# Two DMA issues behind ScalarE's first copies, and one load to the end of its row in SyncE's queue

## The chip, the cores and the metric

The kernel runs on one core of one Trainium2 chip. A core has TensorE (PE, its weight loads shown apart as PEld), VectorE (DVE), ScalarE (ACT), GpSimd (POOL) and SyncE (SP), which work on their own programs and wait for each other by semaphores. DMAs are issued here by SP, ACT and POOL. The metric is the device time of one execution in microseconds (us), the median of several runs.

## The reference

Inputs are `q, k, v, a_re, a_im` of shape (4, 8, 768, 48), that is batch, heads, steps and head size, and two weights of a gated layer. The first half is linear attention with a complex decay per step and channel:

```
a    = (a_re + i*a_im) * min(|a|, 0.999) / (|a| + 1e-6)
S_t  = a_t * S_(t-1) + k_t v_t^T          (S is 48 x 48 per head, complex)
y_t  = q_t . Re(S_t)
```

The second half takes `x = y` as 3072 rows of 384 and computes `h = x @ w_in` (384 x 2048), `g = h * cos(h)` and `g @ w_out` (2048 x 384). The output is 3072 x 384 in float32. The weights come as 64-bit floats and are converted on the chip.

## The kernel before

The 3072 steps are 24 chunks of 128 steps, and two chunks are one group (`G = 2`), so there are 12 groups. Within a chunk the decay is turned into sums: the logarithms of the magnitudes (`lg`) and the angles (`tan`, later the phases) are summed along the steps by a product with a triangular matrix (`p_powers`, `g_phase`). The exponentials of the sums are the powers `P` and `Q = 1/P`. Keys are multiplied by `Q` and queries by `P`, and both by the cosine and the sine of the phase (`p_apply`, `g_stack`): these are the turned keys `ks` and queries `qs`, 96 wide. Then the chunk is ordinary attention: scores of `ks` and `qs`, masked by the causal triangle (`f_scores`, written to `atm`), times `v`, plus the queries times the `state` carried from the chunk before (`f_rows` or `f_out`). The state of the next chunk is `sp`, the keys times the values (`state_sums`), scaled by the chunk's last power (`state_next`).

That last power is called the *end*. It is the last row of `P` in a tile that has steps as partitions, and it is needed with channels as partitions. `row_out` writes the row (3 KB) to a buffer in DRAM by one DMA, and `row_back` reads it back into `end` by two DMAs, the upper and the lower 48 partitions, element by element. For group 0 ACT's queue issues all three (`scalar` in the calls), for later groups SP's. `p_end` scales `end` on DVE and folds it into the test value `least`; `state_next` then uses it.

For groups 0 and 1, `f_turn` turns keys and queries on PE by transposes into a bank of PSUM (`tp`, four heads each), and ACT copies each bank out to `kT` or `qT`. `turn(g, i)` does four of these for one chunk: two for `kT` and two for `qT`. From group 2 on, DVE's block transposes and SP's DMAs do this instead.

The weights are converted in pieces: POOL's queue issues a DMA into `raw`, ACT scales the low words (`lows`), and DVE does three steps per piece (`piece`). The gated layer of a group follows as `hp` (first product), `gate` (cosine and product) and `op` or `sum` (second product).

The order of the instructions: for PE, POOL and the special functions of ACT the order is that of the program text throughout. For DVE and the rest of ACT, including what ACT's queue issues through `scalar`, it is that of the text through the opening of the kernel (`Ordered.by_hand = "vector", "scalar"`); a helper records each such instruction, which is why many have line 676, 687 or 707. The instructions of SP's queue are ordered by a scheduler, unless `behind(a, b)` puts `a` after `b` on their common engine without a wait. The loads of the opening (`load`, line 584) are recorded without such an order, and so is the constant `sums_turned`, which POOL's `exact` is copied from. Each group's `re`, `im`, `k` and `q` share one buffer per name, while `v` has two.

```
DMA             before: waits for the landing of        after: waits for the landing of
v(0) a, b       re(0) a, im(0) a                        re(0) a, im(0) a
sums_turned     v(0) b                                  re(0) b
row<-lg         k(0) b                                  q(0) a
end<-row, 1st   row, v(1) a                             row, v(0) b
end<-row, 2nd   v(1) b                                  im(1) a
```

The opening around the change runs: logarithms and powers of group 0 by halves, `row_out`, phases, `row_back`, turned keys and queries of both chunks, `turn(0, 0)`, `lows(0, 1)`, `piece(0)`, scores of chunk 0, `turn(0, 1)`, scores of chunk 1, and then the logarithms of group 1 interleaved with the rest of group 0.

## Time and profile before

| | us |
|---|---|
| median of 3 runs (657.73 to 659.49) | 657.82 |
| the profiled execution | 657.8 |
| its span, first to last instruction | 656.0 |
| PE busy | 641.3 (98%) |
| DVE busy | 492.4 (75%) |
| ACT busy | 392.5 (60%) |
| POOL busy | 32.0 (5%) |
| granted clock of TensorE, mean | 0.998 |

Times in the traces count from the start of the span. In a timeline each line has start, length, engine, line of the kernel, operation, output and input tiles, shape and count; in brackets stands how long the engine was idle before it, and what ended that. `SPq` and `ACTq` are the issues of SP's and ACT's queues: their length is that of the issue, not of the transfer. The chain of waits is followed back from the last instruction, at each step to what released it. PE's busy time counts overlapped matrix products and is no measure of its peak.

### The profile page before, as it was taken

To read this page: it belongs to the slowest core of one execution; us is meant where nothing else is said; L and a number is where in the kernel's file an instruction comes from. 1 tells how busy PE (TensorE), PEld (TensorE's weight loads), DVE (VectorE), ACT (ScalarE), POOL (GpSimd) and SP (SyncE) were. 2 spreads that over 40 slices of the span, in tenths; PEclk is the share of its full clock that TensorE was granted. 3 is DMA by queue.
4 is the path that set the end of the run, shared out by engine and by line. 5 is a ranking of instruction groups with operands and counts; after the bars stand their busy time and mean duration, and the time that the engine had idled before them with its cause. 6 is when DMAs were issued, how large, how long until landed. Compare 5 with 4: busy or idle time off the path is not lost.

```text
span 656.0 us, 10759 instructions
## 1 busy us (share of the span) xinstructions
PE 641.3 (98%) x4075; PEld 575.7 (88%) x4075; DVE 492.4 (75%) x799; ACT 392.5 (60%) x726; POOL 32.0 (5%) x53
## 2 busy tenths in 40 slices
PE   8899999999999999999999999999999999999996
PEld 5688867777999899899899899899899999999996
DVE  6899989878687688786787777876877878862251
ACT  7788687293583594494585485485476476433330
POOL 4010100000000010010010010000000000000000
PEclk9999999999999999999999999999999999999999
DMA  9969664727626757737838736836936853364001
GB/s 239 224 187 219 196 189 102 190 60 181 145 49 151 186 135 157 193 98 167 217 78 182 206 92 160 207 95 133 245 104 133 224 127 94 112 135 119 25 1 31
DMA packets 232920, 94.90 MB, mean 145 GB/s; under 512 B 208701, under 2 KB 221246, under 8 KB 232858
## 3 DMA queue, kind: packets, MB, share of 16 engines
q1 hardware_dynamic: 225320, 68.51, 45.9%
q0 software_dynamic: 5824, 25.50, 11.9%
q8 instruction: 34, 0.56, 0.4%
q10 hardware_dynamic: 1714, 0.11, 0.2%
q14 instruction: 28, 0.23, 0.1%
HBM read 69.28 MB, written 24.81 MB: 143 GB/s over the span
## 4 chain that ended last, share of the span: by engine, by line
PE 86%; DMA 6%; SPq 2%; DVE 2%; ACT 2%; issue 1%; ACTq 0%; DVEq 0%
PE hp L687 34%; PE op L687 16%; PE sum L687 15%; PE sc L687 6%; PE yp L687 6%; PE sp L687 4%; DMA v<-in_v_dram 2%; PE phs L687 2%; SPq L584 1%; DMA xT<-x 1%; PE lgs L687 1%; DMA qT<-moved 1%; DMA x<-yT 1%; PE yr L687 1%; SPq L936 1%
## 5 line engine op out<-in xcount | busy, mean ns | idle before, releaser
L687 PE MATMUL hp<-xT,w_in 128*128 128x256 f32 (+1 forms) x1176 | 252.7, 376 | 1.0 <-DMA xT<-x 1.0
L687 PEld LDWEIGHTS hp<-xT,w_in 128*128 128x128 f32 x1176 | 219.9, 190 | 31.5 <-DMA xT<-x 0.9
L707 ACT ACTIVATE gate<-hp,half_pi_b 128x512 f32<-128x512 f32 x96 | 66.0, 687 | 120.2 <-PE hp L687 120.2
L676 DVE TENSOR_TENSOR gate<-hp,gate 128x512 f32<-128x512 f32 x96 | 65.7, 685 | 47.2 <-ACT junk L676 47.1
L687 PE MATMUL op<-w_out,gate 128*128 128x192 f32 (+1 forms) x448 | 100.7, 375 | 0.0
L687 PEld LDWEIGHTS op<-w_out,gate 128*128 128x128 f32 x448 | 76.0, 190 | 16.8 <-issue 2.0
L676 ACT ACTIVATE junk<-hp 128x512 bf16<-128x512 f32 x96 | 56.6, 590 | 0.0
L687 PE MATMUL sum<-t_s,s 128*128 128x192 f32 x320 | 56.3, 329 | 0.0
L687 PEld LDWEIGHTS sum<-t_s,s 128*128 128x128 f32 x320 | 52.1, 190 | 1.5 <-issue 1.5
L676 DVE TENSOR_TENSOR atm<-sc,causal 128x512 f32<-128x512 f32 x48 | 32.9, 688 | 25.7 <-PE sc L687 25.6
L687 PEld LDWEIGHTS sc<-qT,kT 96*128 96x128 f32 x384 | 47.2, 192 | 5.4 <-ACT qT L676 2.5
L687 PE MATMUL sc<-qT,kT 96*128 96x128 f32 x384 | 49.2, 277 | 2.5 <-ACT qT L676 2.3
L676 ACT ACTIVATE ot<-sum 128x192 f32<-128x192 f32 x40 | 12.8, 322 | 52.8 <-PE sum L687 52.6
L676 DVE SCALAR_TENSOR_TENSOR ot<-op,ot 128x192 f32<-128x192 f32 x41 | 13.6, 353 | 39.5 <-PE op L687 37.9
L687 PE MATMUL yp<-atm,v 128*48 128x128 f32 x352 | 33.6, 277 | 0.9 <-ACT Q L707 0.6
L703 ACT ACT_TABLE_LOAD x24 | 30.8, 1283 | 1.1 <-PEq L1657 0.7
L687 PE MATMUL yp<-qT,state 96*48 96x128 f32 x304 | 29.7, 272 | 0.0
L687 PE MATMUL sum<-w_out,gate 128*128 128x192 f32 x160 | 29.7, 330 | 0.0
L687 PE MATMUL sp<-v,ks 128*96 128x48 f32 x320 | 29.7, 246 | 0.0
L687 PEld LDWEIGHTS sp<-v,ks 128*96 128x96 f32 x320 | 29.6, 165 | 0.0
L676 ACT COPY yT<-yp 48x512 f32<-48x512 f32 x44 | 25.2, 573 | 7.4 <-PE yp L687 6.9
L676 ACT CAST tan<-phs 128x384 int32<-128x384 f32 x24 | 11.4, 482 | 29.4 <-PE phs L687 29.4
(145 smaller groups left out, 985.7 us busy)
## 6 DMA issues: line engine op xcount, KB each, us to landing
moved<-tr SPq DMA_DIRECT2D x20, 768.0 KB
raw<-in_moe_w_in_dram POOLq DMA_DIRECT2D x16, 768.0 KB, 5.3
raw<-in_moe_w_out_dram POOLq DMA_DIRECT2D x16, 768.0 KB, 4.9
kT<-moved SPq DMA_DIRECT2D x40, 192.0 KB
qT<-moved SPq DMA_DIRECT2D x10, 768.0 KB
k<-in_k_dram SPq DMA_DIRECT2D x24, 192.0 KB
q<-in_q_dram SPq DMA_DIRECT2D x24, 192.0 KB
v<-in_v_dram SPq DMA_DIRECT2D x24, 192.0 KB
```

The lines of the kernel that those rows point to most:

```text
L584: put(out=tile_[lo:hi, i_], in_=steps[lo + by:hi + by, i_])
L676: ins = getattr(self.engine, op)(**kw)
L687: chain(nc.tensor.matmul(out, **kw), "tensor")
L703: chain(nc.scalar.preload_act_table_set(table))
L707: chain(nc.scalar.activation(func=func, **kw))
L936: nc.sync.dma_start(out=X[g][name][:, ds(i * H, n * H), q4], in_=moved[q4])
```

## The change

In ACT's program the two `end<-row` issues of group 0 move from between the last sine of group 0 and the first `kT` copy to behind the four copies of `turn(0, 0)`, ahead of the two `raw` activations of `lows(0, 1)`. In SP's program the two loads of `v` of group 1 move from behind `v` of group 0 to behind `q` of group 1; `sums_turned` then stands ahead of `im` of group 1 instead of behind `re`. The order on PE, DVE and POOL is the same as before. No instruction is added and none is removed.

```diff
-    load(1, ("re", "im", "k", "q", "v"))
+    load(1, ("re", "im", "k", "q"), put=lambda **kw: late.update(load=nc.sync.dma_start(**kw)))
+    load(1, ("v",), put=lambda **kw: behind(nc.sync.dma_start(**kw), late["load"]))
     ones = constant(sums_np[1], "sums_turned", nc.sync, stage["pool"])
...
     g_trig(0, 1, 1)
-    row_back(0, 0, G, scalar)
     busy(10)
     g_stack(0, 0, 1)
     p_apply(0, 1, 1)
...
     turn(0, 0)
+    row_back(0, 0, G, scalar)
     lows(0, 1)
     piece(0)
```

## The prediction

> **What bounds the kernel now.** I read the page first: PE is busy for 98% of the span, so only an idle stretch of PE, or of what feeds it, is worth anything. I then looked at who waited for whom on PE. The longest single wait of the run, after which nothing is left to make it up, is 2.3 us before the first scores `sc`. Then came the chain of waits in order of time, for the stretch that leads to it:

> ```profile
> 10.88 12.75 DMA v<-in_v_dram
> 23.63 0.02 issue
> 23.65 0.31 ACTq L676
> 23.96 0.04 issue
> 24.00 1.07 ACT kT L676 x2
> 25.06 0.50 ACT qT L676
> 25.56 0.04 issue
> 25.60 2.05 PE sc L687 x16
> ```

> The columns are start and length in us. The start of the kernel hangs on a load of values (`v`), then on a DMA that ACT's own queue issues (`ACTq`), then on ACT's copies of the turned keys and queries, then on PE's scores. The timeline of the same stretch names them:

> ```profile
> 21.30 1.08 PE L948 MATMUL tp<-ident,ks 128*96 128x128 f32 x8 [0.22 <-DVE ks L676]
> 22.24 1.08 PE L948 MATMUL tp<-ident,qs 128*96 128x128 f32 x8
> 22.93 1.02 ACTq L676 DMA_DIRECT2D end<-row  x2
> 24.00 1.07 ACT L676 COPY kT<-tp 96x512 f32<-96x512 f32 x2 [3.01 <-DMA v<-in_v_dram]
> 24.96 1.08 ACT L676 COPY qT<-tp 96x512 f32<-96x512 f32 x2
> 25.91 1.91 ACT L676 ACTIVATE raw<-raw,carrier_b 128x768 uint32<-128x768 uint32 x2
> 26.80 0.69 DVE L676 TENSOR_TENSOR atm<-sc,causal 128x512 f32<-128x512 f32 x1 [1.33 <-PE sc L687]
> 27.69 0.69 DVE L676 TENSOR_TENSOR atm<-sc,causal 128x512 f32<-128x512 f32 x1 [0.20 <-PE sc L687]
> 28.13 1.07 ACT L676 COPY kT<-tp 96x512 f32<-96x512 f32 x2 [0.31 <-PE tp L948]
> 34.79 0.96 DVE L676 SCALAR_TENSOR_TENSOR mag<-re,mag 128x768 f32<-128x768 f32 x1 [0.21 <-ACT mag L707]
> 35.91 0.56 DVE L676 TENSOR_SCALAR lg<-lg 128x768 f32<-128x768 f32 x1 [0.15 <-ACT rs L707]
> ```

> The transposes `tp` of chunk 0 are ready from about 21.9, yet ACT copies them only at 24.00: the two `end<-row` issues stand ahead of the copies in its program. In the built program each DMA of SP and ACT takes one of eight completion semaphores in turn and waits for the DMA that had it before. So the first `end<-row` waits for the written row and for half of the second group's values, and the second one for the other half, which the profile names as releaser. How long such a load takes is read from the packets by queue. In the stretch from 18 to 19 us (packets, MB, share of 16 engines):

> ```profile
> q0 software_dynamic: 101, 0.35, 94.5%
> q1 hardware_dynamic: 102, 0.02, 10.3%
> ```

> q0 is POOL's weights, q1 SP's loads. While the weights move, until about 20.7, SP gets some 100 small packets a us; from 21.0 to 21.5 it got 617. A load has 1024 (128 partitions by 8 heads).

> [...] the row's packets pass between 20.6 and 20.8 and its reader starts at 22.93; the second half of `v` passes its last packet near 21.9 (12,429 packets by 22.0; it is the 12th load, ending at 12,288) and releases at 23.63, which is 1.75 us. [...] the `row<-lg` issue starts at 16.95, ahead of the `below` activation of 17.15 that precedes it in the program.

> **Part one, `row_back` behind `turn(0, 0)`.** It adds nothing; two DMA issues move past four copies.
> - ACT's copies: for chunk 1, when ACT waited for PE, the copy started 0.64 us after the first transpose (27.49 to 28.13). So the first copy goes to 21.30 + 0.64 = 21.94. Two copies take 0.96 (24.00 to 24.96), so the first `qT` starts at 22.90 (its transposes allow 22.24 + 0.64 = 22.88), ACT is free at 23.86, and `sc` starts 0.64 after that `qT` as now (24.96 to 25.60): 23.54. **Gain on PE: 25.60 - 23.54 = 2.06 us.**
> - The two issues, 0.31 us each: the first needs the row (22.9 as now) and the first group's values (tenth load, packets passed by 12.0). The second needs, after the change, the first half of `im` of group 1. That is issued at 13.95 in both (DVE reads the old `im` until 13.85). With no `v` ahead of it, it sends perhaps 500 packets by 20.7 at the shared rate, and the other 520 at 617 per 0.5 us take 0.4: last packet 21.2, landed 22.95. If the copies only stand in ACT's queue, both issues run at 22.9 to 23.4 beside them and cost nothing. If the issues follow the last copy in time, they take two times 0.31 plus two gaps of 0.04, 0.7 us. I take nothing; the trace shows this for one queued instruction only, so I keep both ends.
> - Behind them stand `raw` (two, 1.91) and the copies of chunk 1. At nothing: `raw` 23.9 to 25.8; chunk 1's transposes follow `sc` on PE at 27.49 - 2.06 = 25.43, so the copies start at 26.07, and all of ACT moves by 2.06. At 0.7: `raw` ends at 23.86 + 0.7 + 1.91 = 26.47, and ACT moves by 28.13 - 26.47 = 1.66.
> - DVE: it is idle 1.33, 0.20, 0.12 (31.55 to 31.67), 0.21 and 0.15 between 25.5 and 35.9, 2.01 in all; after 36.4 it works without a gap to 62. Its work from 24.91 cannot come sooner, so these gaps are what it can give. The first `atm` can start at 25.4 (instead of 26.80), the second at 26.0, the conversion behind it at 26.65 instead of 28.30 (1.65); the three later gaps close to about 2.06, since successive starts leave 0.05 to 0.1 more than the ends show. So DVE just follows ACT, with hardly a margin.
> - The ends themselves: scatters of 2 x 768 four-byte packets. They pass now by 27.1 (1,557 of q10 by 27.0), landed near 29. They are issued at the same time or 0.4 us later; DVE's `end` scaling, the first reader, moves from 33.75 to 31.7. Over 2 us remain.
> - From 36 on every wait is on another engine of the same core, and PE is full from 62: the gain goes through to the end. I take off 0.05 for the margin on DVE: **-2.0 us**.

> **Part two, the second group's `v` behind its `q`.** The same bytes in another order; the sums for `exact` now also stand ahead of `im`. `v` is first read by chunk 2's `sp` at 66.18; all loads of group 1 have passed by 32.0, so it lands near 34, and 30 us hide it. In SP's queue it now inherits the waits of `k` and `q` (DVE's reads at 22.65 and 23.1) and of `re`; what is queued behind it, the third group's `v`, is issued at 40.66 and waits for PE. `exact` on POOL comes earlier, but POOL's next weights wait for DVE at 30.98 anyway: nothing. The real effect is cover: `re` of group 1 is the 16th load, its last packet passes at 26.1 (16,297 by 26.0) and it lands near 27.85. ACT will want it at 30.04 - 2.06 = 27.98, so part one alone would have 0.1 us to spare. With `v` out of the way it lands about two loads (1.8 us) sooner. Worth: 0, as cover. Done alone, it would give at most the 0.7 us by which 22.95 is earlier than 23.63.

> **Sum.** The profiled execution took 657.8 us (span 656.0 and 1.8 around it), the median of the three runs is 657.82, so either base serves: 657.8 - 2.0 = 655.8. A difference of 0.3%, 1.97 us, is about what a measurement of this kernel can tell from none, and my number lies at that edge.

> **Rivals.**
> 1. ACT pays for the issues, or `im` is late. For it: only one case of running ahead is seen. If `im` came no sooner than its present packets (13,312th near 22.8, landed 24.55), the second issue ends at 24.86, `raw` at 26.8, a move of 1.35. Against: two loads fewer ahead of it. Gain 1.35 to 1.7: 656.1 to 656.5.
> 2. DVE becomes the bound: if its gaps don't close after 28.30, the move stays at 1.65, or at 1.4 if the first `atm` sets it: 656.15 to 656.4. For it: no slack. Against: ACT, not DVE, ended the later gaps.
> 3. Almost nothing arrives, because group 1's logarithm waits for `re` or a later transfer at a fixed time absorbs it: 657 to 657.8. Against: none of the later waits on PE exceeds 1 us.
> 4. Slower: the scatter of `end` meets the next weights. POOL's next load is issued near 29. If 768 of its packets were still waiting then, they would go at the 100 a us seen above, 7.7 us. It would land near 31 + 7.7 + 1.75 = 40.4; DVE, in order, would stand from 31.7 until then, 8.7 us, and the net is 8.7 - 2.0 = +6.7: 664.5. It decides once packets pass later than 29.9; slower than now once they pass later than 32. Against: 27.1 now.

> **How the numbers follow.** The main case (gain 1.85 to 2.15) has 0.60, of which 0.45 over the edge of 1.97 and 0.15 under; rivals 1 and 2 have 0.24, rival 3 has 0.07, rival 4 has 0.05, and 0.04 goes to a gain beyond 2.15. Faster by over 0.3%: 0.49. Within: 0.46. Slower: 0.05. The range of 655.2 to 657.0 takes the main case, rivals 1 and 2, and the noise of the times, and leaves out rival 4, most of rival 3 and the extremes. The main case alone is 655.6 to 656.0.

> **What would show it.** Right: first `kT` copy near 21.9 waiting for PE, `sc` near 23.5, both `end<-row` issues between 22.9 and 24.1, ACT's `lg<-re` of group 1 near 28.0, DVE without a gap until `mag`, `tp` of group 1 near 60.4 instead of 62.48. Wrong: a wait of `raw` or of the copies of chunk 1 on a DMA; DVE waiting before its `end` scaling; `lg<-re` waiting for `re`.

## The result, and the profile after

The changed kernel takes **656.2 us** (median of 22 executions, 654.63 to 661.0), the kernel before, measured beside it, 658.6. The ratio is 0.9968, with a 95% interval of 0.9956 to 0.9981: 2.1 us less (the medians lie 2.4 apart). A repetition, told below, gave 0.9970 (0.9954 to 0.9986). The profiled execution took 655.07 us, with a span of 653.2.

The chain of waits of the changed kernel in the opening (start and length in us). The load of `v` and the `ACTq` issue, which stood ahead of the first copies, are gone from it:

```profile
20.73 0.95 DVE ks L676 x2
21.72 0.66 PE tp L948 x4
22.40 1.07 ACT kT L676 x2
24.01 2.05 PE sc L687 x16
26.06 1.75 PE tp L948 x16
```

The timeline of the same stretch, in the columns that were used for the kernel before:

```profile
21.72 1.08 PE L948 MATMUL tp<-ident,ks 128*96 128x128 f32 x8 [0.22 <-DVE ks L676]
22.40 1.07 ACT L676 COPY kT<-tp 96x512 f32<-96x512 f32 x2 [1.00 <-PE tp L948]
23.36 0.59 ACT L676 COPY qT<-tp 96x512 f32<-96x512 f32 x1
23.84 0.34 ACTq L676 DMA_DIRECT2D end<-row  x1
23.84 0.60 ACT L676 COPY qT<-tp 96x512 f32<-96x512 f32 x1
24.21 0.62 ACTq L676 DMA_DIRECT2D end<-row  x1
24.01 2.05 PE L687 MATMUL sc<-qT,kT 96*128 96x128 f32 x16 [0.27 <-ACT qT L676]
24.88 1.93 ACT L676 ACTIVATE raw<-raw,carrier_b 128x768 uint32<-128x768 uint32 x2 [0.44 <-issue]
26.72 1.04 ACT L676 COPY kT<-tp 96x512 f32<-96x512 f32 x2
28.62 0.84 ACT L749 ACTIVATE lg<-re 128x768 f32<-128x768 f32 x1
33.34 0.96 DVE L676 SCALAR_TENSOR_TENSOR mag<-re,mag 128x768 f32<-128x768 f32 x1 [0.22 <-ACT mag L707]
60.89 1.08 PE L948 MATMUL tp<-ident,ks 128*96 128x128 f32 x8 [0.41 <-DVE ks L676]
```

In the kernel before, the lines for `sc` and for the `tp` of group 1 are:

```profile
25.60 2.05 PE L687 MATMUL sc<-qT,kT 96*128 96x128 f32 x16 [2.28 <-ACT qT L676]
62.48 1.08 PE L948 MATMUL tp<-ident,ks 128*96 128x128 f32 x8 [0.41 <-DVE ks L676]
```

The first `kT` copy now waits for PE and no longer for a DMA, and `sc` waits 0.27 us instead of 2.28. The whole opening starts 0.42 us later in this execution (first `tp` at 21.72 instead of 21.30), because a load of the first group (`im`) came later (ACT's `tan` waits 0.8 us for it instead of 0.3); so the stretches are compared from the first `tp` on. Counted so, the first `kT` copy moved from 2.70 to 0.68, `sc` from 4.30 to 2.29, and the `tp` of group 1 (here and below that of its second chunk, the last line), behind which PE is full, from 41.18 to 39.17: 2.02, 2.01 and **2.01 us** less. Behind this point the fourteen profiled executions below need between 591.5 and 595.1 us more to their ends, whichever kernel it is. So the time of a single execution can't show a gain of 2 us; the position in the opening and the medians can.

The same positions for every kernel that was run (us after the first `tp`, one profiled execution each; "half clock" is explained below):

| kernel | first `kT` copy | `sc` | `raw` | `lg` of group 1 | `tp` of group 1 | half clock in the opening |
|---|---|---|---|---|---|---|
| before | 2.70 | 4.30 | 4.61 | 8.74 | 41.18 | no |
| before_again | 2.63 | 4.24 | 4.55 | 10.22 | 42.79 | yes |
| before_third | 2.27 | 3.87 | 4.18 | 9.92 | 42.43 | yes |
| after | 0.68 | 2.29 | 3.16 | 6.90 | 39.17 | no |
| after_again | 0.68 | 2.29 | 3.15 | 6.88 | 39.17 | no |
| after_third | 0.68 | 2.34 | 3.32 | 7.04 | 39.22 | no |
| e1_ends_only | 0.68 | 2.29 | 3.90 | 7.63 | 39.80 | no |
| e2_values_only | 1.31 | 2.92 | 3.23 | 7.36 | 39.80 | no |
| e3_ends_behind_raw | 0.68 | 2.35 | 2.68 | 6.80 | 39.24 | no |
| e6_behind_raw_values_first | 0.68 | 2.29 | 2.60 | 6.92 | 39.17 | no |
| e4_ends_late | 0.68 | 2.29 | 2.59 | 7.21 | 39.53 | no |
| e7_ends_last | 0.68 | 2.29 | 2.60 | 6.73 | 42.68 | yes |
| e9_last_filled | 0.68 | 2.28 | 2.59 | 6.72 | 46.57 | yes, longer |
| e8_before_filled | 2.38 | 3.99 | 4.30 | 8.43 | 40.87 | no |

### The profile page after: what moved, and what is told of

Same layout as the page of the kernel before. It is cut to its first block, busy times and chain, and to the rows that moved or that the text cites. A ratio compares the mean times of both kernels' runs of the same rounds, so it can differ in the third digit from the quotient of the medians.

```text
span 653.2 us, 10758 instructions
## 1 busy us (share of the span) xinstructions
PE 641.3 (98%) x4075; PEld 575.9 (88%) x4075; DVE 491.8 (75%) x799; ACT 392.8 (60%) x726; POOL 30.9 (5%) x53
## 4 chain that ended last, share of the span: by engine, by line
PE 86%; ACT 6%; DMA 4%; DVE 3%; issue 1%; SPq 0%; DVEq 0%; ACTq 0%
PE hp L687 37%; PE op L687 17%; PE sum L687 14%; PE sc L687 5%; PE yp L687 5%; PE sp L687 4%; PE phs L687 2%; DMA qT<-moved 1%; ACT tan L707 1%; PE lgs L687 1%; ACT rs L707 1%; DMA raw<-in_moe_w_in_dram 1%; PE yr L687 1%; ACT L703 1%; PE tp L948 1%; ACT lg L707 1%
## 5 line engine op out<-in xcount | busy, mean ns | idle before, releaser
L687 PE MATMUL hp<-xT,w_in 128*128 128x256 f32 (+1 forms) x1176 | 252.6, 375 | 0.3 <-DMA xT<-x 0.3
L687 PEld LDWEIGHTS hp<-xT,w_in 128*128 128x128 f32 x1176 | 219.6, 190 | 30.8 <-issue 0.7
L707 ACT ACTIVATE gate<-hp,half_pi_b 128x512 f32<-128x512 f32 x96 | 66.0, 688 | 119.1 <-PE hp L687 119.1
L687 PE MATMUL op<-w_out,gate 128*128 128x192 f32 (+1 forms) x448 | 100.7, 374 | 0.0
L676 DVE TENSOR_TENSOR gate<-hp,gate 128x512 f32<-128x512 f32 x96 | 65.6, 683 | 46.3 <-ACT junk L676 46.2
L687 PEld LDWEIGHTS op<-w_out,gate 128*128 128x128 f32 x448 | 75.9, 190 | 16.9 <-issue 2.0
L676 ACT ACTIVATE junk<-hp 128x512 bf16<-128x512 f32 x96 | 56.7, 591 | 0.0
L687 PE MATMUL sum<-t_s,s 128*128 128x192 f32 x320 | 56.3, 329 | 0.0
L687 PEld LDWEIGHTS sum<-t_s,s 128*128 128x128 f32 x320 | 52.1, 190 | 1.5 <-issue 1.5
L676 DVE TENSOR_TENSOR atm<-sc,causal 128x512 f32<-128x512 f32 x48 | 32.9, 689 | 23.2 <-PE sc L687 23.1
L687 PEld LDWEIGHTS sc<-qT,kT 96*128 96x128 f32 x384 | 47.4, 192 | 2.8 <-issue 0.9
L687 PE MATMUL sc<-qT,kT 96*128 96x128 f32 x384 | 49.0, 276 | 0.5 <-ACT qT L676 0.3
L676 ACT ACTIVATE ot<-sum 128x192 f32<-128x192 f32 x40 | 12.8, 322 | 53.6 <-PE sum L687 53.4
L676 DVE SCALAR_TENSOR_TENSOR ot<-op,ot 128x192 f32<-128x192 f32 x41 | 13.7, 353 | 40.1 <-PE op L687 38.5
L687 PE MATMUL yp<-atm,v 128*48 128x128 f32 x352 | 33.6, 277 | 0.9 <-ACT Q L707 0.6
L687 PE MATMUL yp<-qT,state 96*48 96x128 f32 x304 | 29.7, 272 | 0.0
L687 PE MATMUL sum<-w_out,gate 128*128 128x192 f32 x160 | 29.7, 329 | 0.0
L687 PE MATMUL sp<-v,ks 128*96 128x48 f32 x320 | 29.7, 245 | 0.0
L687 PEld LDWEIGHTS sp<-v,ks 128*96 128x96 f32 x320 | 29.6, 165 | 0.0
L676 ACT COPY yT<-yp 48x512 f32<-48x512 f32 x44 | 25.2, 573 | 7.3 <-PE yp L687 6.9
L676 ACT CAST tan<-phs 128x384 int32<-128x384 f32 x24 | 11.4, 481 | 29.3 <-PE phs L687 29.3
```

The costliest lines, as they stand in the source:

```text
L676: ins = getattr(self.engine, op)(**kw)
L687: chain(nc.tensor.matmul(out, **kw), "tensor")
L707: chain(nc.scalar.activation(func=func, **kw))
```

## The experiments

The theory to be tested: the issues stood in front of the copies and waited for a load; the order of the copies gives all of the gain, and the order of the loads is only cover. The rival: the order of the loads has a worth of its own, since it decides what the issues wait for. Ratios are to the kernel before on the same chip, with their 95% interval.

**One part of the change at a time.** `e1_ends_only` is the kernel before with the issues moved and the loads left:

```diff
-    row_back(0, 0, G, scalar)
     busy(10)
...
     turn(0, 0)
+    row_back(0, 0, G, scalar)
```

> Part one alone: row_back behind turn(0, 0), the loads as before. Theory on record (part two is only cover): the full gain, 655.8 to 656.2 against 657.8 to 658.6, ratio 0.997; sc 2.3 us after the first tp (4.30 before, 2.29 in the changed kernel). Rival (part two is what keeps the issues from stalling ACT): in this build the second end<-row waits for the second half of im of group 1, which with v ahead of it is the 14th load (14,336th packet, near 23.9 in the trace of before, landed near 25.6). Then sc still starts 2.3 us after the first tp, but raw starts no earlier than in the kernel before (25.9), ACT's lg of group 1 only 0.3 us earlier, and the total gains 0.3 to 0.6 us: ratio 0.999.

`e2_values_only` is the kernel before with the loads moved and the issues left:

```diff
-    load(1, ("re", "im", "k", "q", "v"))
+    load(1, ("re", "im", "k", "q"), put=lambda **kw: late.update(load=nc.sync.dma_start(**kw)))
+    load(1, ("v",), put=lambda **kw: behind(nc.sync.dma_start(**kw), late["load"]))
```

> Part two alone: v of group 1 behind q, row_back where it was. In this build the two end<-row issues wait for the row and for the two halves of v of group 0, which landed long before. Theory: the row is then the last to come, landed near 22.9 as before, the issues end near 23.6, the first kT copy starts 0.4 us earlier against the first tp (2.3 instead of 2.70 after it), and the total gains 0.3 to 0.5 us, ratio 0.9993. Rival (the row was late only because im blocks SP's issues and the row's descriptors behind them): the row lands near 20, the copies start as soon as PE has finished, and the gain is the full 2.0 us, ratio 0.997.

Measured: e1 656.7 us, ratio 0.9974 (0.9962 to 0.9986); e2 656.2 us, 0.9965 (0.9953 to 0.9976). By the position of the `tp` of group 1 each part alone gives 41.18 - 39.80 = 1.38, and both together 2.01, not 2.76. The times don't tell the three apart: the intervals of e1, of e2 and of the whole change overlap, and e2's median is that of the change. ACT's timeline of e1:

```profile
23.30 0.37 ACTq L676 DMA_DIRECT2D end<-row  x1
24.64 0.39 ACTq L676 DMA_DIRECT2D end<-row  x1
25.08 1.94 ACT L676 ACTIVATE raw<-raw,carrier_b 128x768 uint32<-128x768 uint32 x2 [1.18 <-DMA im<-in_a_im_dram]
```

and of e2:

```profile
21.70 0.91 ACTq L676 DMA_DIRECT2D end<-row  x2
22.65 1.07 ACT L676 COPY kT<-tp 96x512 f32<-96x512 f32 x2 [1.63 <-PE tp L948]
```

In e1 the copies run at once, but the second issue waits for a half of `im` of group 1, with which it shares a completion semaphore, and `raw` stands behind it for 1.18 us. In e2 both issues run from 21.70, for 0.91 us, and the copies only wait until these are done. So each part takes away most of the wait by itself: the one puts the copies in front of it, the other gives the issue earlier loads to wait for. The rival was right, and "cover only" was wrong. Both numbers expected of e2 were off: `kT` comes 1.31 us after `tp`, where 2.3 was expected by the theory and the full gain by its rival.

e2 shows a second thing. Its first issue needs the written row, as in the kernel before, and it starts at 21.70. The row's packets pass between 20.6 and 21.0, so it is there at most 1.1 us after its first packet. In the kernel before the row's packets passed at the same time (20.6 to 20.8) and the issue started only at 22.93. So what it waited for then was not the row; by the table of semaphores it was the first half of `v` of group 1.

The packets fit that. By 33.0, SP's 20 loads and `sums_turned` make 20,944 packets, which is 1,040 for each load (1,024 and 16 more) and 144 for `sums_turned`. The first half of `v` is the 11th load and ends at 11,440, near 21.2 (11,192 by 21.0, 11,809 by 21.5), 1.7 us ahead of the first issue. The second half ends at 12,480, just after 22.0, 1.6 us ahead of the second issue.

**What the issues cost ACT.** In the changed kernel `raw` starts 0.44 us late, with "issue" as the reason, behind two issues that take 0.96 us. If that counts, putting the issues behind `raw` should give something more. `e3_ends_behind_raw` does so with the new order of the loads, `e6_behind_raw_values_first` with the old one:

```diff
     turn(0, 0)
-    row_back(0, 0, G, scalar)
     lows(0, 1)
+    row_back(0, 0, G, scalar)
     piece(0)
```

> The changed kernel with row_back one step later, behind the two raw activations. In the changed kernel ACT was idle 0.44 us for the issues ahead of raw. Theory (that idle time is later absorbed where ACT waits for PE anyway): ACT's lg of group 1 starts about 0.2 us earlier against the first tp (6.7 instead of 6.90), but the second tp of group 1 stays at 39.2 us after the first, and the total is that of the changed kernel within 0.1 us, ratio to before 0.997. Rival (ACT still sets the pace): another 0.2 to 0.4 us off, ratio 0.9964.

> Part one taken one step further (row_back behind the two raw activations) and part two left out: v of group 1 again ahead of re and im. In this build the first end<-row waits for the row and for the second half of im of group 1, the second for nothing more. Theory after the first four runs (an issue holds only what stands behind it in ACT's program, and with values first it is im that it waits for, landed 3.5 us after the first tp): raw starts 2.6 us after the first tp, the issues run beside it, the copies of chunk 1 start about 4.9 us after the first tp, and the second tp of group 1 comes 39.2 us after it as in the changed kernel: ratio to before 0.9967, so part two isn't needed. Rival (the values must be out of the way, because re or im come too late for ACT's logarithm of group 1): lg waits for a DMA and the second tp comes 39.8 after the first, as in part one alone: ratio 0.9977.

Measured: e3 656.1 us, 0.9964 (0.9950 to 0.9979); e6 655.8 us, 0.9971 (0.9958 to 0.9984). ACT's timeline of e3, then of e6:

```profile
23.68 1.00 ACTq L676 DMA_DIRECT2D end<-row  x2
24.14 1.95 ACT L676 ACTIVATE raw<-raw,carrier_b 128x768 uint32<-128x768 uint32 x2
26.34 1.07 ACT L676 COPY kT<-tp 96x512 f32<-96x512 f32 x2 [0.25 <-PE tp L948]
```

```profile
24.02 1.95 ACT L676 ACTIVATE raw<-raw,carrier_b 128x768 uint32<-128x768 uint32 x2
25.46 0.93 ACTq L676 DMA_DIRECT2D end<-row  x2
26.43 1.07 ACT L676 COPY kT<-tp 96x512 f32<-96x512 f32 x2 [0.46 <-PE tp L948]
```

`raw` comes 0.5 us sooner than in the changed kernel (2.68 and 2.60 after `tp` instead of 3.16), and the `tp` of group 1 stands where it did (39.24 and 39.17 instead of 39.17). Most of the 0.44 us that the issues cost is lost in time in which ACT would have waited for PE: e3's next copy waits 0.25 us for it, that of the changed kernel follows without a wait. In e3 the `lg` of group 1 is 0.10 us earlier than in the changed kernel (6.80 after `tp` instead of 6.90), and this tenth does not reach the `tp` of group 1. e6 also shows that the order of the loads is not needed where the issues stand behind `raw`: they start at 25.46, 4.04 us after `tp`, and the half of `im` that held up e1's second issue had landed 3.46 us after `tp` there. The gain is the same 2.01.

**How late may the ends come?** My rival for "slower" was that the reads of the ends meet POOL's next weights. `e4_ends_late` puts the issues behind `turn(0, 1)` (the first diff), `e7_ends_last` just ahead of the scaling of `end` (the second), both with the new loads:

```diff
     turn(0, 1)
+    row_back(0, 0, G, scalar)
     piece(0, 1, 0, 1)
```

```diff
     f_scores(1, 1)
+    row_back(0, 0, G, scalar)
     p_end(0, 0, 2)
```

> The changed kernel with row_back behind all eight copies (behind turn(0, 1)), so that the two issues run near 28.5 instead of 24. This is the slower rival put to the test. If scatters meet the weights: POOL's next raw load is issued near 29.5 and sends from 31; the 1,536 packets, which took 2 us from their first, would start near 30 and share the engines for their second half: landed 34 to 38 instead of 29.5, DVE stands still before its end scaling (32.3 in the changed kernel) for 2 to 6 us, and the total is 0 to 4 us above the kernel before. If the scatter gets through ahead of the weights: landed near 33.5, a stall of 1.2 us, total gain left 0.8 us. If the ends have slack of any size: same as the changed kernel.

> The changed kernel with row_back as late as it can stand, just ahead of p_end and behind the logarithm and first exponential of group 1 in ACT's program, so that the scatters (issued near 31) meet POOL's weights, which send from 31 to 34. Theory: SP's small packets got 100 a us beside weights, and 600 to 700 a us of the scatters pass without them, so some 300 pass by 34 and the rest by 36: landed 36 to 38, DVE stands still before its end scaling (due at 32.3) for 4 to 6 us, and the net over the kernel before is a loss of 2 to 4 us, ratio 1.003 to 1.006. Rival (small scatters get through beside weights): landed near 34.5, a stall of 2 to 2.5 us, net within 0.5 us of the kernel before, ratio 0.9995 to 1.0005.

Measured: e4 656.7 us, 0.9977 (0.9958 to 0.9996); e7 660.6 us, **1.0055** (1.0034 to 1.0076). DVE's timeline of e4, then ACT, DVE and PE of e7:

```profile
33.04 0.17 DVE L676 TENSOR_SCALAR end<-end 96x16 f32<-96x16 f32 x1 [0.85 <-DMA end<-row]
```

```profile
32.05 0.91 ACTq L676 DMA_DIRECT2D end<-row  x2
35.06 0.17 DVE L676 TENSOR_SCALAR end<-end 96x16 f32<-96x16 f32 x1 [3.12 <-DMA end<-row]
35.96 0.42 PE L687 MATMUL yr<-state,qT 96*128 96x48 f32 x2 [1.69 <-DVE state L676]
37.89 2.87 PE L687 MATMUL hp<-xT,w_in 128*128 128x128 f32 x12
42.31 1.57 PE L687 MATMUL hp<-xT,w_in 128*128 128x128 f32 x12
```

In e4 the issues run at 27.34 to 28.32, and DVE waits 0.85 us for the data; the `tp` of group 1 is 0.36 us later than in the changed kernel. The data come 4.7 us after the second issue (28.32 to 33.04). Between 28.0 and 31.0, 1,536 of the 1,568 packets pass, beside 691, 952 and 896 packets of SP's loads in the three us. The last 32 pass only between 31 and 32, when POOL's weights have begun (31 packets in this us). What holds these back, the loads or the weights, was not tested. The expectation for a scatter that gets through ahead of the weights (landed near 33.5, a stall of 1.2 us) is the one that e4 comes near. Another cost shows in e4's times: 9 of its 22 executions have a mean clock below 0.998 and a median of 659.7, the other 13 have 656.2.

In e7 the issues run only at 32.05 to 32.96. Most of the small packets pass between 33.5 and 34.5, after the weights: 1,226 of the 1,232 weight packets had gone by 33.5, and then 720 small ones followed in half a us. So the ends land about 2.1 us after the second issue, and the collision with weights hardly took place in e7 (305 small packets and 40 of weights pass between 33.0 and 33.5); what DVE waits for is the late issue, 3.12 us. PE waits 1.69 us of these.

That alone takes back less than the 2.01 that the copies bring, and yet the kernel is slower than before. The last two lines say why: 12 `hp` products take 2.87 us at 37.89, and 1.57 at 42.31. TensorE's clock was halved there: the windows of 1 us from 37 to 41 have 0.59, 0.50, 0.50 and 0.70, which is 1.71 us of missing work. With the wait this makes 1.69 + 1.71 = 3.40 of the 3.51 us by which the `tp` of group 1 is later than in the changed kernel. The profiled execution is e7's fastest (657.36 us); the others lose more, with mean clocks down to 0.988. The ratio is the one that the theory of a collision gave (1.003 to 1.006), but it came by another way; that agreement is luck.

**The clock.** The kernel before and the changed one were profiled once more:

> The kernel before once more, for a second profile. Theory (the wait for v is steady): first kT copy 2.5 to 3.0 us after the first tp, sc 4.1 to 4.6 after it, second tp of group 1 41.0 to 41.5 after it. If the wait for v depends on how DMAs happen to interleave, these differ by over 0.5 us from the first profile (2.70, 4.30, 41.18).

> The changed kernel once more, for a second profile: first kT copy 0.68 us after the first tp, sc 2.3 after it, ACT idle 0.4 us ahead of raw, second tp of group 1 39.2 after the first tp.

`after_again` took 656.2 us and repeats the positions. `before_again` took 659.9 us; its `kT` and `sc` stand where they were expected, its `tp` of group 1 does not, for behind the wait of `sc` its transposes run at nearly half speed. Its PE timeline, then its windows of 1 us (stretch, length, PE busy and count, granted clock, DMA share, GB/s):

```profile
25.68 2.08 PE L687 MATMUL sc<-qT,kT 96*128 96x128 f32 x16 [2.22 <-ACT qT L676]
27.57 1.90 PE L948 MATMUL tp<-ident,ks 128*96 128x128 f32 x8
29.25 1.89 PE L948 MATMUL tp<-ident,qs 128*96 128x128 f32 x8
```

```profile
27.00:28.00 1.00, 1.00 (x10) 0.79 1.34 217
28.00:29.00 1.00, 1.00 (x6) 0.50 1.22 225
29.00:30.00 1.00, 1.00 (x7) 0.50 0.48 82
30.00:31.00 1.00, 1.00 (x7) 0.51 0.76 155
```

The missing clock adds up to 0.21 + 0.50 + 0.50 + 0.49 = 1.70 us of work, and the `tp` of group 1 stands 42.79 - 41.18 = 1.61 us later than in the first profile of the kernel before, which had a clock of 1.00 from the start to 652. So the wait that the change takes away may cost twice.

The timed executions point the same way, since each comes with its mean clock. In the first profiles of the kernel before and of the changed kernel the clock is also halved at the very end, from 2.1 and 3.4 us behind the last product on, where nothing waits for it; in the ten profiles whose opening is undisturbed, the mean is 0.998 to 1.000. Of the kernel before, 88 of 145 executions (in three sets) have less than 0.998; of the changed kernel, 5 of 44 (in two). A mean of 0.997 lies at the edge between the two; at 0.996 or less stand 66 of the 145 and 2 of the 44.

To test it, `e8_before_filled` is the kernel before with work that nobody reads put into PE's wait, and `e9_last_filled` is e7 with such work in its wait (the second diff):

```diff
     turn(0, 0)
+    busy(7)
     lows(0, 1)
```

```diff
     f_columns(0)
+    busy(6)
     f_rows(1, 0, HH)
```

> The kernel before with seven products of the idle tile put on TensorE between the transposes of chunk 0 and the first scores (about 0.27 us each, 1.9 us of the 2.3 us wait; their result is read by nobody). Theory: the wait costs twice, as the wait itself, and because TensorE's clock is halved behind it in some executions. 62 of the 102 timed executions of the kernel before show a mean clock under 0.998, with a median of 659.2, the other 40 have 657.0. Filled, sc starts about 4.3 after the first transposes and the second tp of group 1 about 41.2 after them, as in the first profile of before, with a clock of 1.00 from 26 to 31; nearly all executions have 0.998 or more, the median is near 657.2, the ratio near 0.998. Rival: the lower clock has another cause (the executions differ in something else), then the median stays within 0.3 of before and as many executions have the lower clock.

> The changed kernel once more, beside the filled one. Ratio to before near 0.997. Against the filled kernel: if the whole wait taken away by the change (2.0 us in the trace) counts, it is 2.0 below it; if what the two groups of executions of before suggest is right (657.05 at the higher clock against 656.2), only 0.9.

> The kernel before once more, one profile. Of its executions about 6 in 10 have the lower mean clock; so either a stretch at half clock behind the 2.2 us wait ahead of sc and the second tp near 42.8 after the first transposes, or none and 41.2. A third pattern would speak against the two groups.

> The kernel with the ends' issues just ahead of p_end, with six products of the idle tile put on TensorE ahead of the rows of chunk 1, where it waited 1.69 us for the state. Theory: what made that kernel slower than before is the halved clock that followed (hp x12 took 2.87 instead of 1.57, the yr rows some 0.3 more). Filled, these durations are 1.57 and as before, the second tp of group 1 stands near 41.1 after the first transposes instead of 42.7, the mean clock is 0.998 or more in most executions, and the ratio is 0.998 to 1.000. Rival: the wait for the ends alone makes it slower: the ratio stays near 1.005.

Measured, on one chip: before 658.4 us, e8 657.7, changed kernel 656.15 (ratio 0.9970, 0.9954 to 0.9986). e8's own ratio is 0.9991 with an interval of 0.9980 to 1.0002, so its time alone doesn't prove the point. The clock speaks more plainly: 12 of 14 executions of e8 have 0.998 or more, against 17 of 43 of the kernel before; none of e8 has 0.996 or less, against 24 of 43; and e8's slowest took 658.5 where before's took 664.5. PE's timeline of e8, then of `before_third`, with its windows:

```profile
23.27 1.86 PE L687 MATMUL busy<-idle 128*128 128x512 f32 x7
25.49 2.05 PE L687 MATMUL sc<-qT,kT 96*128 96x128 f32 x16 [0.35 <-ACT qT L676]
27.38 1.04 PE L948 MATMUL tp<-ident,ks 128*96 128x128 f32 x8
```

```profile
25.24 2.92 PE L687 MATMUL sc<-qT,kT 96*128 96x128 f32 x16 [1.85 <-ACT qT L676]
27.96 1.86 PE L948 MATMUL tp<-ident,ks 128*96 128x128 f32 x8
```

```profile
26.00:27.00 1.00, 1.00 (x8) 0.61 1.34 195
27.00:28.00 1.00, 1.00 (x7) 0.50 1.35 230
28.00:29.00 1.00, 1.00 (x6) 0.50 1.29 208
29.00:30.00 1.00, 1.00 (x9) 0.69 1.27 216
```

In e8 `sc` comes when the wait lets it, as in the kernel before, yet runs and is followed at full clock (1.00 in each us from 24 to 31). `before_third` has half clock behind a wait of 1.85 us, shorter than the 2.2 that was expected, and its `tp` of group 1 stands at 42.43 instead of 42.8.

So of the 658.41 - 656.15 = 2.26 us that the change gives by the medians, about 658.41 - 657.73 = 0.7 are the clock behind the wait and 1.6 the wait itself. The 1.6 is less than the 2.0 of the first profile, and both numbers of the expectation (2.0 and 0.9) were off. The split is rough: e8's interval leaves anything from nothing to 1.3 us for the clock, and the 17 executions of the kernel before with 0.998 or more have a median of 657.19, which would make it 1.2 of clock and 1.0 of wait. The table shows one reason why the wait is less than 2.0: the first `kT` copy of a kernel with the wait stands 2.70, 2.63, 2.27 or 2.38 after `tp`, since its time hangs on a load and that of `tp` does not; less 0.68, the wait is worth 2.02, 1.95, 1.59 or 1.70.

e9 took 658.55 us, 1.0006 (0.9995 to 1.0018), where e7 had 1.0055, and 10 of 15 executions have a clock of 0.998 or more, where none of the 12 of e7 had. That speaks for the theory and against the stall as the only cause, though the ratio is a little above what I expected. Its profiled execution is its slowest, 664.0 us, and does not show what was expected (the `tp` of group 1 near 41.1, at full clock): the ends came 0.76 us later still, PE waited 1.03 us in spite of the filling, and the clock was halved all the same, until 49, though PE is shown busy in every us of that time. Why it stayed halved so long is open:

```profile
36.72 0.42 PE L687 MATMUL yr<-state,qT 96*128 96x48 f32 x2 [1.03 <-DVE state L676]
```

```profile
38.00:39.00 1.00, 1.00 (x10) 0.90 0.06 16
39.00:40.00 1.00, 1.00 (x7) 0.50 0.00 0
```

## Why the prediction was right, and where it was not

The forecast was 655.8 us and 656.2 was measured; the gain of 2.0 us is one of 2.1 by the ratio. That agreement is partly luck, as the steps show.

- **Part one, the copies: right.** `kT` 0.64 after the first transposes was forecast and is 0.68; `sc` 2.24 and is 2.29; the gain on PE 2.06 and is 2.01.
- **The two issues: between the two ends of the bound.** The first of them ran beside the last copy, both from 23.84; but the second ran until 24.83, and `raw` started 0.44 late. ACT's `lg` moved by 8.74 - 6.90 = 1.84 us, where 2.06 and 1.66 stood. The forecast of nothing holds for the end of the chain, by another way than the one that was told: ACT did stand, mostly in time in which it would otherwise have waited for PE.
- **DVE just follows: right.** Its three gaps between 26.8 and 32 closed, and small ones stayed (0.22 us ahead of `mag`, 0.15 ahead of `lg`), so ACT and not DVE still set the pace, and rival 2 was wrong.
- **The ends: right.** DVE's `end` at 32.30 waits for nothing. e4 shows where the margin stops: issued 4.0 us later (6.13 after `tp` instead of 2.12), the ends cost DVE 0.85 us.
- **Part two, worth 0: this step failed.** Alone it gives 1.38 us where "at most 0.7" stood. The 0.7 rested on the row as releaser of the first issue at 22.93. I took the row as landed only then, 2.1 us behind its last packets (20.8), because the issue that needs it starts there, and that only fitted by chance: e2 issues at 21.70, 0.7 us behind its row's packets (21.0). The releaser was `v` of group 1. The packets were also misread by 16 for each load: the second half of `v` ends at 12,480 and not at 12,288, and `re` of group 1 at 16,640, after 26.0 (16,297) by about half a us.
- **Part one alone would give all of it: this failed too.** I had worked out the semaphores of the whole change, but not those of part one alone; e1's second issue waits for `im` and loses 0.6 us. The reason that I gave for cover (`re`, with 0.1 us to spare) was not the one that counted: in e6, with the loads in the old order, `lg` runs 6.92 after `tp` and no wait for `re` is shown.
- **Rival 1** had the right kind of event (an issue that waits for `im`), but in e1 and not in the changed kernel. **Rival 3** was wrong: the 2.01 us reached the `tp` of group 1 whole. **Rival 4** took its price from the wrong event. Late ends do make the kernel slower, by 0.55% in e7, but through the late issue and the clock; in e7 the packets were hardly held up by weights, and in e4 this is open for the last 32.
- **The sum: right in size, wrong in what it holds.** It treated the wait as 2.0 us and the clock as given. By the medians it is about 1.6 us of wait and 0.7 us of clock, a rough split; that part is the clock is shown by the filling, how much is not. The base was mis-sized too: 657.8 (three runs and one profile) against 658.0 to 659.0 in the larger sets, because most executions of the kernel before have the lower clock and the profiled one had not.

## What to carry to other kernels

An issue of a DMA is an instruction that waits (in e1 `raw` stood 1.18 us behind one): find what it shares a completion semaphore with in the built program, for the order that you mean to build and for each half of it, and put the issue where those loads have landed (here behind `raw`, where the order of the loads stopped mattering). Price a wait of PE of about 2 us not only by its length, but also by the clock of what follows (0.50 behind the waits of 1.69, 1.85 and 2.22 us here, 1.00 behind that of 2.28), and take two or three profiles before a base is trusted. Whether a wait costs the clock can be tested by filling it with products that nobody reads.

## What the runs showed of the hardware that I had not expected

**TensorE's clock was halved behind short waits.** It fell to 0.50 behind waits of 2.22 us (before_again), 1.85 (before_third) and 1.69 (e7), and behind one of 1.03 in e9. The missing clock is 1.70 us in before_again and in before_third and 1.71 in e7, which is 3.40 and 3.42 us at half clock. In e9 5.12 us are missing (38 to 50 us), which is 10.24, three times as long. The first profile of the kernel before waited 2.28 us and kept its clock (1.00 in each us from 17 to 31).

Why the same wait costs the clock in some executions and not in others was not shown. The time without products ahead of the fall differed at the end of the two first profiles, too: in the kernel before the last product is done at 650.84 us and the clock falls to half at 652.94, 2.1 us later; in the changed kernel at 647.77 and 651.16, 3.4 us later.

**ACT's queue issued DMAs past instructions that stand ahead of them.** In e3 both issues start at 23.68, before the two `raw` activations that precede them in the program (24.14 to 26.09). The prediction had seen it for one instruction (`row<-lg`, 0.20 us ahead of `below`). In the other direction it wasn't free: the instruction behind an issue didn't start until the issue was done (0.44 us of idle time ahead of `raw` in the changed kernel, 0.36 ahead of `lg` in e4), and the issue of e1 that waited for a load held `raw` for 1.18 us.

**Reads of four bytes passed quickly.** The two reads of `end` are 1,536 packets of four bytes. In e7, behind the weights, 720 small packets passed in half a us (33.5 to 34.0). In the changed kernel it was 658 (26.0 to 26.5), with 342 packets of SP's loads beside them. The 102 packets a us that SP's loads got beside the weights are thus not the rate of such reads once the weights are through.
